# A static plan re-priced: new costs for small vector work, two due times and a buffer limit in a fused attention and MLP kernel

## The chip, the cores and the metric

One core of one Trainium2 chip. The metric is the device time of one execution in microseconds, the median over several runs. Engines are named as in the profile: PE is TensorE (PEld its weight loads), DVE VectorE, ACT ScalarE, POOL GpSimd, SP SyncE, which issues nearly all DMAs.

## The reference

Block-causal attention over 8 batches, 8 heads, 576 positions in blocks of 64, head size 64, followed by layer norm, a two-layer MLP with ReLU and a residual, all in float32:

```python
scores = scale * np.matmul(q, k.transpose(0, 1, 3, 2))
scores = np.where(block_i >= block_j, scores, -1000000000.0)
attn = softmax(scores); attn_out = np.matmul(attn, v)
x = attn_out.transpose(0, 2, 1, 3).reshape(8, 576, 512)
xn = (x - mu) / np.sqrt(var + 1e-06) * g_ln
out = x + np.maximum(xn @ w_ch1, 0.0) @ w_ch2      # 512 -> 2048 -> 512
```

## The kernel before

**Attention.** 32 pairs of heads, four to a batch (`pair`). The first block of 64 rows is kept out of a pair; the other 512 rows are four tiles of 128. A pair's PE work is: scores into PSUM (L416), transposes of the exponentials (L446), products with v (L452, L456). Between them DVE scales, masks and writes the scores to SBUF and finds each row's extreme in one instruction (L434, tiles `pu` for row tiles 1 and 2, `pab` for 3 and 4), ACT takes exp with row sums (L437), and ACT or DVE evacuates the transposes (`evac`, `copy` at L234 and L236). DVE transposes the finished rows (`ot`, L530) and SP stores them in `xd`.

**First blocks.** Once in 8 pairs, `first(m)` (m = 0 to 3) does the first blocks of two batches: scores of 64 x 64 (L568, on PE ahead of the scores of pair 8m + 4), maximum and difference on DVE (L576, L578, twice each), exp on ACT (L582), sum and reciprocal on DVE (L586 to L588, one task `total`), a product on POOL (L590), transposes (L597) and products with v (L608) on PE during pair 8m + 5, two transposes on DVE (L615), four stores. It loads `qk0` (L555) and `v0` (L571).

**Weights.** They come as 64-bit words of float64 patterns. `decode` runs 32 times (16 slices, each of both matrices): load `wr` (L345, L347), two ACT steps (L350, L355), a POOL step (L353), two DVE steps (L359, L362), then a store, for the second matrix after a split into a rounded high part and the rest (`wd`: cast at L234 or L236, L373 on POOL).

**Norm and MLP.** 36 row tiles in five rounds of 8, 8, 8, 8 and 4. `norm_tiles` handles two row tiles at a time (index q): load x from `xd`, scale by the softmax sums (L669), mean and variance (L691 in round 0, ACT in the others), reciprocal root (Newton steps on POOL), normalise (L724 in round 0), times g (L727, POOL), transpose (L729) through DRAM to `xt`. `operands` builds seven operand blocks `xm` from each `xt` for a seven-product (Strassen) scheme: differences (L754), casts to the rounded format (at L234 or L236) and remainders (L765). `products` (PE L867, evacuated and combined at L875, L880, L886, L887) and `second` (PE L927, added up at L936) run 8 groups in each round. `x` holds rows in rounds 1 to 4, `x0` in round 0.

**What orders the work.** Each engine runs its instructions in the order in which they are written, and that order comes from a planner (`Plan.run`) that simulates a time line while the kernel is built. Each task has a priority (smaller goes first), a modelled cost for every engine that could take it, and buffers it must find free. The planner takes the ready task with the smallest priority, on an engine only if no other engine would end it sooner, and on DVE and ACT it passes over a task if a task nearer by more than 100 is about to be ready before its modelled end. Pair k has priority 100 + 10k plus 0.05 for each step. PE's order in the attention phase is fixed by a chain of steps instead. Cost functions in us, n elements per partition:

```python
def dve(n):
    return .07 + n / 960
def act(n, sbuf=False):
    return .055 + .085 * sbuf + n / 1200
def pool(n):
    return .07 + n / 440
```

`D_0`, `D_1`, `LN_0`, `LN_1` and `LATER` (top of the file) set due times: decode n has the priority of pair `D_0 + D_1 * n + LATER` = 15 + 0.97n, the norm of round 0 that of pair 13 + 3q, its operands that of pair 25. Their loads wait for gates, the scores of earlier pairs (`ends`), in which LATER does not occur. `small` tiles share 21 buffers of 512 floats per partition, with a limit for each name: ya 10, x 3, t 4, tt 4, xnt 2, mag 2, sgn 2 and others.

Of the kernel before, what the change touches and what calls it, by code (L numbers as in the profile page):

```python
# [27 lines left out]
TILES = sum(ROUNDS)  # L28
D_0, D_1 = 12.0, .97
LN_0, LN_1 = 10, 3  # L30
LATER = 3
AHEAD = 100, 5, .25


# [23 lines left out]
class Plan:  # L58
# [5 lines left out]
    def add(self, eng, cost=None, fn=None, r=(), w=(), prio=0.0, size=0, alloc=(), mode=128):  # L64
        k = Task(eng if isinstance(eng, dict) else {eng: (cost, fn)}, prio, size)
        k.mode = mode
        before = {}
        for x in r:
            before.update(dict.fromkeys(x.writers))
        for x in w:  # L70
            before.update(dict.fromkeys(x.readers))
        for x in r:
            x.readers.append(k)
        for x in w:
            x.writers.append(k)
        for x in before:
            x.next.append(k)
        k.left = len(before)
        k.uses = list(dict.fromkeys(x.root for x in (*r, *w, *alloc)))
        for x in k.uses:  # L80
            x.users += 1
        k.allocs = [x for x in dict.fromkeys(x.root for x in (*w, *alloc)) if x.make]
        self.tasks.append(k)
        return k
# [105 lines left out]
# [6 lines that stand above are left out]


def pool(n):
    return .07 + n / 440

@with_exitstack
def attn_mlp_kernel(ctx: ExitStack, tc: tile.TileContext, qk, qk0, v, v0, w1, w2, g, out):
# [79 lines left out]
    def small(name, shape, dtype, most):  # L282
        return kind(name, shape, dtype, 21, None, "small", most)
# [8 lines left out]
    new_ot, new_v0 = small("ot", [P, 512], F32, 2), small("v0", [P, 512], F32, 1)  # L292
    new_e0, new_pt00, new_ot0 = (small(n, [P, 512], F32, 1) for n in ("e0", "pt00", "ot0"))
    new_mag, new_sgn = (small(n, [P, 512], I32, 2) for n in ("mag", "sgn"))
    new_ya, new_x, new_xnt = (small(n, [P, 512], F32, k) for n, k in (("ya", 10), ("x", 3), ("xnt", 2)))
    new_x0, new_xn = small("x0", [P, 512], F32, 2), small("xn", [P, 512], F32, 1)
    new_t, new_tt, new_sum = small("t", [P, 512], F32, 4), small("tt", [P, 2, 2, P], F32, 4), small("sum", [P, 2, 256], F32, 2)
    xs = [kind(f"xm{p}", [P, max(ROUNDS) // 2, 2, 2, P], F32R, 1)() for p in range(7)]
# [37 lines left out]
    def decode(j, second, prio, gate):  # L336
        n = 512
        wrb, magb, sgnb = new_word(), new_mag(), new_sgn()
        wr, mag, sgn = (lambda x=x: x.t for x in (wrb, magb, sgnb))
        wv = lambda i: wr().rearrange("p (n two) -> p n two", two=2)[:, :, i]  # L340
        word, magn, sign, full = (Buf(parent=x) for x in (wrb, magb, sgnb, sgnb))

        def dma():
            if second:
                nc.sync.dma_start(out=wr(), in_=w2[j])  # L345
            else:
                nc.sync.dma_start(out=wr().rearrange("p (c n) -> p c n", c=NC),  # L347
                                  in_=w1[:, :, 2 * j * P:2 * (j + 1) * P].rearrange("c p n -> p c n"))
        load(P * n * 8, dma, r=gate, w=[word], alloc=[wrb], prio=prio)
        add("ACT", act(n, True), lambda: nc.scalar.activation(  # L350
            out=mag().bitcast(F32), in_=wv(1).bitcast(F32), func=AF.Abs, scale=65536.0), r=[word], w=[magn], prio=prio)
        mag2 = Buf(parent=magb)
        add(any_of(lambda e: e.tensor_scalar_max(mag().bitcast(F32), mag().bitcast(F32), 2.0),  # L353
                   POOL=.07 + n / 367), r=[magn], w=[mag2], prio=prio)
        add("ACT", act(n, True), lambda: nc.scalar.activation(  # L355
            out=sgn(), in_=wv(0).bitcast(U32), func=AF.Copy, scale=2.0 ** -29 * (1 - 2.0 ** -9), bias=-0.499),
            r=[word], w=[sign], prio=prio)
        sign2 = Buf(parent=sgnb)
        add("DVE", dve(n), lambda: nc.vector.scalar_tensor_tensor(  # L359
            out=sgn(), in0=wv(1), scalar=-2147483648, in1=sgn(), op0=ALU.bitwise_and, op1=ALU.bitwise_or),  # L360
            r=[sign, word], w=[sign2], prio=prio)
        add("DVE", dve(n), lambda: nc.vector.scalar_tensor_tensor(  # L362
            out=sgn(), in0=mag(), scalar=3, in1=sgn(), op0=ALU.logical_shift_left, op1=ALU.bitwise_or),
            r=[sign2, mag2], w=[full], prio=prio)
        w = lambda: sgn().bitcast(F32)
        to = (wcs if second else w1f)[j // 2]
        out = Buf(parent=to)
        if second:
            wd = new_wd()
            hi, lo = Buf(parent=wd), Buf(parent=wd)  # L370
            add(any_of(lambda e: copy(e, wd.t[:, 0], w()), ACT=act(n, True), DVE=.12 + n / 1920),
                r=[full], w=[hi], prio=prio)
            add("POOL", pool(n), lambda: nc.gpsimd.tensor_sub(wd.t[:, 1], w(), wd.t[:, 0]), r=[full, hi], w=[lo], prio=prio)  # L373
            load(P * 4096, lambda: nc.sync.dma_start(
                out=to.t[:, 1024 * (j % 2):1024 * (j % 2) + 1024], in_=wd.t.rearrange("p l n -> p (l n)").bitcast(F32)),
                r=[hi, lo], w=[out], prio=prio)
        else:
            load(P * 2048, lambda: nc.sync.dma_start(out=to.t[:, 512 * (j % 2):512 * (j % 2) + 512], in_=w()),
                 r=[full], w=[out], prio=prio)
        whole.setdefault((second, j // 2), []).append(out)  # L380
# [164 lines left out]

    def first(m):

        prio = 100 + 10 * (8 * m + 3)
        step = [0]

        def pr():
            step[0] += 1
            return prio + .05 * step[0]
# [31 lines left out]
        def total():  # L585
            nc.vector.tensor_reduce(out=nm.t, in_=ev(e.t), op=ALU.add, axis=AX.X)  # L586
            nc.vector.tensor_scalar_add(nm.t, nm.t, 1e-9)
            nc.vector.reciprocal(nm.t, nm.t)  # L588
        add("DVE", dve(512) + .4, total, r=[p, *d], w=[r1], prio=pr())
        add("POOL", pool(512), lambda: nc.gpsimd.tensor_mul(  # L590
            ev(e.t), ev(e.t), nm.t.unsqueeze(2).to_broadcast([P, 8, 64])), r=[p, r1], w=[pn], prio=pr())
        tr, pt, turned_ = new_tr(), new_pt00(), Buf()
# [49 lines left out]
    def norm_tiles(n, q, prio, gate):  # L642
# [74 lines left out]
        for h, (x, part) in enumerate(rows):  # L717
            unit, scaled = Buf(parent=x), Buf(parent=x)
            if n:
                add("ACT", act(512, True), lambda x=x, h=h: nc.scalar.activation(  # L720
                    out=x.t, in_=x.t, func=AF.Identity, bias=norm.t[:, 10 + h:11 + h], scale=norm.t[:, 4 + h:5 + h]),
                    r=[rstd], w=[unit, *part], prio=prio)
            else:
                add("DVE", dve(512), lambda x=x, h=h: nc.vector.tensor_scalar(  # L724
                    out=x.t, in0=x.t, scalar1=norm.t[:, 2 * h:2 * h + 1], scalar2=norm.t[:, 4 + h:5 + h],
                    op0=ALU.subtract, op1=ALU.mult), r=[rstd], w=[unit, *part], prio=prio)
            add(any_of(lambda e, x=x: e.tensor_mul(x.t, x.t, g_sb), POOL=pool(512)), r=[unit, gb], w=[scaled], prio=prio)  # L727
            xnt, xw = new_xnt(), new_xw()
            add("DVE", dve(512), lambda x=x, xnt=xnt: nc.vector.transpose(xnt.t, x.t), r=[scaled], w=[xnt], prio=prio)  # L729
            parts = []  # L730
            for g4 in range(4):
                parts.append(Buf(parent=xw))
                load(32 * 2048, lambda xw=xw, xnt=xnt, g4=g4: nc.sync.dma_start(
                    out=xw.t[:, 32 * g4:32 * g4 + 32].rearrange("(k r) q -> r k q", r=32),
                    in_=xnt.t[32 * g4:32 * g4 + 32].rearrange("p (k q) -> p k q", q=32)), r=[xnt], w=[parts[-1]], prio=prio)
            half = Buf(parent=xt)
            load(P * 2048, lambda xw=xw, h=h: nc.sync.dma_start(
                out=xt.t[:, h].rearrange("p (c q) -> p c q", q=P), in_=xw.t.rearrange("(c p) q -> p c q", p=P)),
                r=parts, w=[half], alloc=[xt], prio=prio)
            ready.append(half)  # L740
# [4 lines left out]
    def operands(n, prio):  # L745
# [5 lines left out]

        def diff(p, q, i, in0, in1, r, w):
            new = Buf(parent=tts[q])
            add(any_of(lambda e: e.tensor_sub(tmp(q, i), in0(), in1()), DVE=dve(256), POOL=pool(256)),  # L754
                r=r, w=[new, *w], prio=prio + .1 * p + .01 * q)
            return new

        def split(step, p, q, src, r):
            old = held.get((n - 1, p), [])
            hi, lo = Buf(parent=xs[p]), Buf(parent=xs[p])  # L760
            three = lambda x: x.rearrange("p (c n) -> p c n", c=2)
            pr = prio + .1 * step + .01 * q
            add(any_of(lambda e: copy(e, xs[p].t[:, q, 0], three(src())), ACT=act(256, True), DVE=.08 + 256 / 1920),
                r=r, w=[hi, *old], prio=pr)
            add(any_of(lambda e: e.tensor_sub(xs[p].t[:, q, 1], three(src()), xs[p].t[:, q, 0]),  # L765
                       DVE=dve(256), POOL=pool(256)), r=[hi, *r], w=[lo, *old], prio=pr)
            got.setdefault(p, []).extend((hi, lo))
            return hi, lo

# [242 lines left out]
```

## Time and profile before

| | us |
|---|---|
| three runs | 1049.40, 1050.07, 1050.23 (median 1050.07) |
| the profiled execution's own time | 1050.46 |
| its span in the trace | 1048.7 |
| PE, DVE, ACT, POOL busy | 1037.1, 743.7, 524.0, 286.3 |

The attention phase lasts until about 303 us, the MLP's products from there to the end. The granted TensorE clock is at its full level throughout. Busy time is the time in which an engine has an instruction in work; for PE its ends are modelled, so an instruction that waits in PE's queue can look busy. The span leaves out what lies around the execution, some 1.8 us.

### The profile page before, as it was taken

How to read it: one execution, taken by the hardware profiler on the slowest of the kernel's cores; microseconds unless marked ns; L12 is line 12 of the kernel's file. 1: busy time of each engine (PE TensorE's matmuls, PEld its weight loads, DVE VectorE, ACT ScalarE, POOL GpSimd, SP SyncE). 2: the span in 40 equal slices, each digit the busy share in tenths (PEclk: the TensorE clock that was granted, in tenths of full speed). 3: DMA queues.
4: the chain of work that ended last, by engine and by line, in shares of the span. 5: the costliest groups of instructions: out<-in, count | busy, mean ns of one | idle time of the engine just before them, and what ended most of it. 6: DMA issues, size and time to landing. Idle time of an engine off the chain costs nothing.

```text
span 1048.7 us, 17977 instructions
## 1 busy us (share of the span) xinstructions
PE 1037.1 (99%) x6256; PEld 852.4 (81%) x6256; DVE 743.7 (71%) x1629; ACT 524.0 (50%) x1264; POOL 286.3 (27%) x468
## 2 busy tenths in 40 slices
PE   8999999999999999999999999999999999999998
PEld 7877777777878888888888888888888888888997
DVE  5778999989878878885656684665595555465544
ACT  6999888899875535342433341343242322122221
POOL 0223454545343765340222240222240220000000
PEclk9999999999999999999999999999999999999999
DMA  7578889898779898858777647688657667336873
GB/s 270 200 256 266 222 288 279 234 300 295 261 272 306 276 310 238 251 209 265 217 243 213 231 159 259 186 242 248 183 200 262 207 192 251 139 111 249 299 279 126
DMA packets 237930, 248.91 MB, mean 237 GB/s; under 512 B 159376, under 2 KB 188048, under 8 KB 227600
## 3 DMA queue, kind: packets, MB, share of 16 engines
q1 hardware_dynamic: 237840, 247.77, 72.9%
q8 instruction: 49, 0.80, 0.3%
q14 instruction: 41, 0.34, 0.1%
HBM read 182.71 MB, written 65.01 MB: 236 GB/s over the span
## 4 chain that ended last, share of the span: by engine, by line
PE 90%; DVE 7%; DMA 1%; issue 1%; ACT 0%; SPq 0%; POOL 0%; DVEq 0%; POOLq 0%; ACTq 0%
PE y L927 36%; PE p L867 32%; PE tr L446 7%; PE s L416 7%; PE o L456 5%; PE o L452 2%; DVE pab L434 1%; DMA wc<-wcs 1%; DVE pu L434 1%; DMA x<-xd 1%; DVE sgn L359 0%; DVE x L724 0%; DVE ya L936 0%; DVE xm L765 0%; PE tr L326 0%
## 5 line engine op out<-in xcount | busy, mean ns | idle before, releaser
L927 PE MATMUL y<-wc,h 128*128 128x512 f32 x1728 | 433.8, 390 | 0.2 <-DVE h L887 0.2
L927 PEld LDWEIGHTS y<-wc,h 128*128 128x128 f32 x1728 | 322.1, 188 | 66.4 <-DVE h L887 1.3
L936 DVE TENSOR_TENSOR ya<-y,ya 128x512 f32<-128x512 f32 x288 | 197.6, 687 | 181.6 <-PE y L927 178.8
L867 PE MATMUL p<-xm,wa 128*128 128x512 f32 (+1 forms) x960 | 221.7, 368 | 0.0
L867 PEld LDWEIGHTS p<-xm,wa 128*128 128x128 f32 x960 | 169.9, 188 | 31.5 <-issue 0.2
L867 PE MATMUL p<-xm,wb 128*128 128x512 f32 (+1 forms) x720 | 166.2, 368 | 0.0
L875 ACT COPY t<-p 128x512 f32<-128x512 f32 (+1 forms) x120 | 65.2, 544 | 167.8 <-PE p L867 166.0
L867 PEld LDWEIGHTS p<-xm,wb 128*128 128x128 f32 x720 | 127.7, 188 | 23.7
L886 ACT ACTIVATE h<-t 128x512 fp32r<-128x512 f32 (+1 forms) x120 | 62.2, 579 | 162.5 <-DVE t L880 162.3
L880 DVE TENSOR_TENSOR t<-p,t 128x512 f32<-128x512 f32 (+1 forms) x120 | 76.3, 636 | 47.9 <-PE p L867 43.2
L416 PE MATMUL s<-raw 64*128 64x224 f32 (+3 forms) x768 | 97.2, 388 | 2.5 <-DVE nm L434 2.0
L437 ACT ACTIVATE pab<-pab,nm 128x448 f32<-128x448 f32 (+1 forms) x128 | 91.2, 731 | 0.2 <-DVE nm L434 0.2
L234 ACT COPY pt<-tr 128x512 f32<-128x512 f32 x166 | 87.0, 597 | 7.2 <-PE tr L446 5.8
L416 PEld LDWEIGHTS s<-raw 64*128 64x128 f32 x768 | 74.8, 188 | 18.8 <-issue 5.1
L434 DVE CUSTOM_DVE_ANT_0 pab<-s,never 128x448 f32<-128x448 f32 (+1 forms) x128 | 82.7, 684 | 2.2 <-PE s L416 1.8
L456 PE MATMUL o<-pt,v 128*64 128x256 f32 (+1 forms) x768 | 80.1, 344 | 0.0
L456 PEld LDWEIGHTS o<-pt,v 128*64 128x64 f32 x768 | 55.3, 137 | 27.6
L887 DVE SCALAR_TENSOR_TENSOR h<-t,h 128x512 fp32r<-128x512 f32 (+1 forms) x120 | 74.1, 666 | 3.9 <-ACT h L886 3.8
L353 POOL TENSOR_SCALAR mag<-mag 128x512 f32<-128x512 f32 x32 | 48.7, 1525 | 101.4 <-ACT mag L350 92.4
L681 POOL TENSOR_SCALAR norm<-norm 128x1 f32<-128x1 f32 x28 | 6.9, 245 | 248.5 <-ACT xn L678 248.5
L437 ACT ACTIVATE pu<-pu,nm 128x320 f32<-128x320 f32 (+1 forms) x128 | 64.8, 510 | 19.5 <-DVE nm L434 18.5
L446 PE MATMUL tr<-ident,pab 128*128 128x128 f32 x512 | 63.3, 274 | 3.9 <-DVE nm L434 2.8
(96 smaller groups left out, 1036.3 us busy)
## 6 DMA issues: line engine op xcount, KB each, us to landing
wc<-wcs SPq DMA_DIRECT2D x40, 1024.0 KB, 7.0
wa<-was SPq DMA_DIRECT2D x32, 1024.0 KB, 6.3
wb<-wbs SPq DMA_DIRECT2D x32, 768.0 KB, 5.8
raw<-qk SPq DMA_DIRECT2D x32, 576.0 KB, 4.8
wr<-w SPq DMA_DIRECT2D x32, 512.0 KB, 6.1
v<-v SPq DMA_DIRECT2D x32, 320.0 KB, 5.5
x<-xd SPq DMA_DIRECT2D x144, 64.0 KB, 3.9
xrow<-x SPq DMA_DIRECT2D x36, 256.0 KB, 3.9
```

What stands on the lines that cost most here:

```text
L234: e.copy(out=out, in_=in_)
L416: nc.tensor.matmul(x, raw.t[HALF[h], 0, col], raw.t[HALF[h], 1, at:at + x.shape[1]], start=True, stop=True)
L434: add("DVE", dve(n) + .01, lambda: nc.vector.tensor_tensor_reduce(out=two(p.t[:, part(i, h)]), in0=mine(), in1=two(hide), scale=-0.125, sc ...
L437: add("ACT", act(n, True) + .14, lambda: nc.scalar.activation(out=p.t[:, part(i, h)], in_=p.t[:, part(i, h)], func=AF.Exp, bias=nm.t[:, at ...
L446: nc.tensor.transpose(o.t[:, n * P:(n + 1) * P], x, ident)
L456: nc.tensor.matmul(o.t[HALF[h], at + lo:at + 256], v_sb.t[:, ck, HALF[h]], rhs(h), start=False, stop=(n == len(steps) - 1), skip_group_che ...
L867: nc.tensor.matmul(x.t[:, 0:TN], w_(l), xs[m].t[:, 0:half, o, k], start=start and k == e == 0, stop=k == 1 and e == 2, skip_group_check=True)
L875: add("ACT", act(TN), lambda: nc.scalar.copy(out=t.t[:, 0:TN], in_=x.t[:, 0:TN]), r=[r], w=[new], prio=0)
L880: add("DVE", dve(TN), lambda: nc.vector.tensor_add(t.t[:, 0:TN], x.t[:, 0:TN], t.t[:, 0:TN]), r=r, w=[new], prio=0)
L887: add("DVE", dve(TN), lambda: nc.vector.scalar_tensor_tensor(out=x.t[:, 1, 0:TN], in0=src(), scalar=0.0, in1=x.t[:, 0, 0:TN], op0=ALU.max, ...
L927: nc.tensor.matmul(yb.t, x.t[:, l, at:at + P], wc.t[:, i, o], start=i == e == 0, stop=i == 1 and e == 2)
L936: add("DVE", dve(512), lambda yb=yb, ya=ya: nc.vector.tensor_add(ya.t, yb.t, ya.t), r=[part, before_], w=[now], prio=1)
```

## The change

Three cost functions change or are added (`pool`, `dve2` for DVE work from SBUF, `cast` for DVE casts to the rounded format), the cost of `total` grows, LATER goes from 3 to 2, the limit of `x` buffers from 3 to 4, and `first(m)` takes the priority of pair 8m + 4 in place of 8m + 3. The instructions themselves stay the same.

```diff
-LATER = 3
+LATER = 2
...
 def pool(n):
-    return .07 + n / 440
+    return .1 + n / 390
+def dve2(n):
+    return .1 + n / 760
+def cast(n):
+    return .2 + n / 1400
...
-    new_ya, new_x, new_xnt = (small(n, [P, 512], F32, k) for n, k in (("ya", 10), ("x", 3), ("xnt", 2)))
+    new_ya, new_x, new_xnt = (small(n, [P, 512], F32, k) for n, k in (("ya", 10), ("x", 4), ("xnt", 2)))
...   in decode, both steps (L359, L362)
-        add("DVE", dve(n), lambda: nc.vector.scalar_tensor_tensor(
+        add("DVE", dve2(n), lambda: nc.vector.scalar_tensor_tensor(
...   in first
-        prio = 100 + 10 * (8 * m + 3)
+        prio = 100 + 10 * (8 * m + 4)
...
-        add("DVE", dve(512) + .4, total, r=[p, *d], w=[r1], prio=pr())
+        add("DVE", dve(512) + .8, total, r=[p, *d], w=[r1], prio=pr())
...   in norm_tiles, round 0 (L724)
-                add("DVE", dve(512), lambda x=x, h=h: nc.vector.tensor_scalar(
+                add("DVE", dve2(512), lambda x=x, h=h: nc.vector.tensor_scalar(
...   in operands: diff (L754), the cast (L234, L236), the remainder (L765)
-            add(any_of(lambda e: e.tensor_sub(tmp(q, i), in0(), in1()), DVE=dve(256), POOL=pool(256)),
+            add(any_of(lambda e: e.tensor_sub(tmp(q, i), in0(), in1()), DVE=dve2(256), POOL=pool(256)),
...
-            add(any_of(lambda e: copy(e, xs[p].t[:, q, 0], three(src())), ACT=act(256, True), DVE=.08 + 256 / 1920),
+            add(any_of(lambda e: copy(e, xs[p].t[:, q, 0], three(src())), ACT=act(256, True), DVE=cast(256)),
...
-                       DVE=dve(256), POOL=pool(256)), r=[hi, *r], w=[lo, *old], prio=pr)
+                       DVE=dve2(256), POOL=pool(256)), r=[hi, *r], w=[lo, *old], prio=pr)
```

## Rows read from the trace of the kernel before

**Rows 1.** The page's head and its first part: the span, then busy us of each engine (share of the span) and number of instructions.

```profile
span 1048.7 us, 17977 instructions
PE 1037.1 (99%) x6256; PEld 852.4 (81%) x6256; DVE 743.7 (71%) x1629; ACT 524.0 (50%) x1264; POOL 286.3 (27%) x468
```

**Rows 2.** The order of time on PE in the attention phase: start us, length us, engine, line, operation, tiles, form, number of instructions merged. The row that begins the scores of a pair (L416) is shown for pairs 2, 12, 13, 16, 17, 20, 21, 26, 27 and 31, and the first-block scores (L568) ahead of pair 20.

```profile
19.88 2.86 PE L416 MATMUL s<-raw 64*128 64x320 f32 x24
...
110.25 0.80 PE L416 MATMUL s<-raw 64*128 64x320 f32 x2
...
120.40 2.86 PE L416 MATMUL s<-raw 64*128 64x320 f32 x24
...
148.45 2.86 PE L416 MATMUL s<-raw 64*128 64x320 f32 x24
...
157.19 2.86 PE L416 MATMUL s<-raw 64*128 64x320 f32 x24
...
184.55 0.69 PE L568 MATMUL tr<-qk 64*64 64x64 f32 x32
185.18 3.12 PE L416 MATMUL s<-raw 64*128 64x320 f32 x24
...
196.50 2.86 PE L416 MATMUL s<-raw 64*128 64x320 f32 x24
...
242.99 1.61 PE L416 MATMUL s<-raw 64*128 64x320 f32 x10
...
253.38 2.86 PE L416 MATMUL s<-raw 64*128 64x320 f32 x24
...
291.46 2.86 PE L416 MATMUL s<-raw 64*128 64x320 f32 x24
```

**Rows 3.** The chain of work that ended last, in order of time: start us, length us, engine, tile, line, number of instructions. First the transposes of a first-block job, then three places of the MLP phase.

```profile
124.28 0.44 PE tr L597 x4
...
369.38 2.72 PE y L927 x12
...
410.82 2.72 PE y L927 x12
...
941.22 2.72 PE y L927 x12
```

**Rows 4.** Three stretches: from:to and length us, then busy us (and instructions) of PE, PEld, DVE, ACT and POOL, the granted clock, the DMA engines' share and GB/s.

```profile
100.00:275.00 175.00, 170.08 (x1642) 133.43 (x1640) 161.61 (x479) 155.29 (x423) 84.10 (x118) 1.00 0.88 273
275.00:303.00 28.00, 28.00 (x282) 22.72 (x278) 21.93 (x65) 26.72 (x73) 8.38 (x7) 1.00 0.61 204
...
350.00:402.00 52.00, 51.82 (x228) 42.41 (x227) 45.89 (x71) 25.00 (x49) 34.73 (x40) 1.00 0.90 268
```

**Rows 5.** The order of time on DVE around the first-block jobs 1 and 2 (columns as in rows 2).

```profile
112.10 0.69 DVE L576 TENSOR_REDUCE nm<-tr 128x4 f32<-128x256 f32 x2
...
185.73 0.75 DVE L576 TENSOR_REDUCE nm<-tr 128x4 f32<-128x256 f32 x2
186.40 0.74 DVE L578 TENSOR_TENSOR e<-tr,nm 128x256 f32<-128x256 f32 x2
...
188.59 0.64 DVE L586 TENSOR_REDUCE nm<-e 128x8 f32<-128x512 f32 x1
...
190.05 0.13 DVE L539 TENSOR_SCALAR sums_all<-sums_all 128x32 f32<-128x32 f32 x1
...
191.06 0.45 DVE L434 CUSTOM_DVE_ANT_0 pu<-s,never 128x320 f32<-128x320 f32 x1
```

**Rows 6.** The order of time on DVE around the operand work of pair 25 and 26.

```profile
236.80 0.69 DVE L359 SCALAR_TENSOR_TENSOR sgn<-wr,sgn 128x512 int32<-128x512 int32 x1
237.40 0.62 DVE L434 CUSTOM_DVE_ANT_0 pab<-s,never 128x448 f32<-128x448 f32 x1
...
237.95 0.49 DVE L236 CAST xm<-xt 128x256 fp32r<-128x256 f32 x2
...
241.78 0.74 DVE L434 CUSTOM_DVE_ANT_0 pab<-s,never 128x576 f32<-128x576 f32 x1
```

**Rows 7.** First-block job 1 in the order of time on POOL and on PE; and the line of its `qk0` loads on SP: number, shortest/median/longest ns, first and last start us.

```profile
115.73 1.04 POOL L590 TENSOR_TENSOR e<-e,nm 128x512 f32<-128x512 f32 x1 [2.52 <-ACT pt L234]
...
124.12 0.60 PE L597 MATMUL tr<-ident,e 128*128 128x128 f32 x4
...
L555 SPq DMA_DIRECT2D qk<-qk x4: 328/427/795, 3.3 to 180.4; - x4
```

**Rows 8.** Groups of instructions by line and form: busy us, mean ns of one, idle before them. The two casts are those of 20 to 303 us; the next row is the work on `xm` alone from 100 to 275 us (columns as in rows 4); then the decode's first DVE step over the whole span.

```profile
L236 DVE CAST xm<-tt 128x256 fp32r<-128x256 f32 x12 | 5.1, 429 | 0.0
L236 DVE CAST xm<-xt 128x256 fp32r<-128x256 f32 x12 | 3.6, 332 | 0.0
...
100.00:275.00 175.00, 0.00 (x0) 0.00 (x0) 13.42 (x35) 1.54 (x4) 13.66 (x17) 1.00 0.88 273
...
L359 DVE SCALAR_TENSOR_TENSOR sgn<-wr,sgn 128x512 int32<-128x512 int32 x32 | 25.4, 795 | 1.7 <-ACT sgn L355 1.7
```

**Rows 9.** The page's DMA issues: tiles, queue, number, size, median us from issue to landing.

```profile
x<-xd SPq DMA_DIRECT2D x144, 64.0 KB, 3.9
```

**Rows 10.** The order of time on DVE and on POOL at 108 us.

```profile
108.57 3.19 POOL L727 TENSOR_TENSOR x<-x,g_sb 128x512 f32<-128x512 f32 x2 [1.59 <-DVE x L724]
108.86 1.76 DVE L359 SCALAR_TENSOR_TENSOR sgn<-wr,sgn 128x512 int32<-128x512 int32 x1
```

More of the change, by code (lines that the diff above doesn't have):

```diff
@@ L358, in decode @@
         sign2 = Buf(parent=sgnb)
-        add("DVE", dve(n), lambda: nc.vector.scalar_tensor_tensor(
+        add("DVE", dve2(n), lambda: nc.vector.scalar_tensor_tensor(
             out=sgn(), in0=wv(1), scalar=-2147483648, in1=sgn(), op0=ALU.bitwise_and, op1=ALU.bitwise_or),
             r=[sign, word], w=[sign2], prio=prio)
-        add("DVE", dve(n), lambda: nc.vector.scalar_tensor_tensor(
+        add("DVE", dve2(n), lambda: nc.vector.scalar_tensor_tensor(
             out=sgn(), in0=mag(), scalar=3, in1=sgn(), op0=ALU.logical_shift_left, op1=ALU.bitwise_or),
```

## The prediction

> **What bounds the kernel now.** I read the page first: TensorE (PE) is busy in nearly the whole span, so time can only be won where PE stands still or runs slower than its own pace [rows 1]. Busy time hides such places, since a matmul that waits inside its queue still counts. So I read the order of time on PE next and compared the starts of the score matmuls of successive pairs [rows 2]. A plain pair takes 157.19 - 148.45 = 8.74 us. A first-block job adds about 2.2 us to the pairs around it: 0.63 from its start to the next scores (185.18 - 184.55), twice 0.26 for scores that run 3.12 instead of 2.86, 0.44 for its transposes [rows 3], and for its values as much again as for its scores. From pair 2 (19.88) to pair 31 (291.46) that makes 29 x 8.74 + 4 x 2.2 = 262.3 us; the trace has 271.6. **About 9.3 us of waiting are in the attention phase.**
>
> In the MLP phase the chain of waits shows PE at an even pace: from 410.82 to 941.22 are exactly 26 x 20.40 us. Only from 369.38 to 410.82 it is 41.44, 0.64 over two periods [rows 3]. So the change can win 9.9 us at most, and not from rounds 1 to 4.
>
> What PE waits for is read from the stretches: from 100 to 275 us VectorE (DVE) is busy 161.6 of 175 us, ACT 155.3, POOL only 84.1 [rows 4]. Each engine runs in written order, so the wait is for whatever the planner put on DVE ahead of a softmax. The order of time on DVE shows two kinds. Behind the scores of pair 20 stand two L576 and two L578 (185.73 to 187.1) and L586 to L588 (188.59 to 190.05), between norm work, and the softmax of that pair starts at 191.06 [rows 5]; that interval is 196.50 - 185.18 = 11.32, less 8.74 + 0.26: 2.3 us lost. Job 1 likewise comes at 112.10 ahead of pair 12's softmax [rows 5], and 120.40 - 110.25 - 9.00 = 1.15 us are lost [rows 2]. The other kind is rounding and splitting of the MLP's operands: two casts at 237.95 open a run of them that ends at 241.78, where the pab softmax resumes [rows 6]; pair 26 takes 253.38 - 242.99 = 10.39, 1.65 too long [rows 2]. The remaining 9.3 - 2.3 - 1.15 - 1.65 = 4.2 us are smaller waits among the same work.
>
> **The change part by part.** No arithmetic is added or taken away. The parts are prices of the planner, two due times and a buffer limit.
>
> First-block job from 8m + 3 to 8m + 4. Old, its DVE steps were ahead of everything of pair 8m + 4 and of what was left of pair 8m + 3 (its evacuations and the ot transpose). New, they stand level with pair 8m + 4: by step numbers the two L576 and one L578 come before the third and fourth pu softmax, L586 to L588 after the third. So the leftovers and part of the softmax go first. What it can give is at most the two waits, 2.3 + 1.15 = 3.45; I take half for the part that stays in front, 1.7. At worst it costs: the job's POOL product ends at 116.8 and its transposes on PE start at 124.12 in a fixed place of PE's order [rows 7], 7.3 us of cover; a full pair later (8.74) would miss by 1.4, in four jobs 5.8. Level is not a full pair, so I take no loss. Its qk0 loads are issued at 3.3 to 180.4 us [rows 7]; the last of them, for job 3, goes out before job 2 has started (184.55, [rows 2]), eight pairs ahead of its use, so a delay of 10 priority units, one pair, is hidden. The v0 load and the four stores of its rows are moved past other SP work too; those rows belong to tiles 8, 17, 26 and 35, which no norm of round 0 reads, and the MLP covers them. Its one POOL product moves by no more than the DVE steps.
>
> Cast 256 from 0.213 to 0.383 us, ACT still 0.353. Between idle engines the planner now takes ACT. In the attention phase 24 of 28 of these casts ran on DVE, 5.1 + 3.6 = 8.7 us, and 4 on ACT at 1.54 / 4 = 0.385 us [rows 8]; ACT has 175 - 155.3 = 19.7 us idle in its busiest stretch [rows 4]. Moving half frees DVE of 4.3 us just in the runs that delay pair 26. Prices dve2 for the decode, the norm scaling and the operand differences (512: 0.603 to 0.774, 256: 0.337 to 0.437) and pool (512: 1.234 to 1.413) make the planner count 2 x 0.17 us more per decode and more room around each; the decode's first step has a mean of 0.795 [rows 8] and two POOL products beside it 3.19 / 2 = 1.6 [rows 10], so both come nearer. First-block total: 1.003 to 1.403, in the trace 190.05 - 188.59 = 1.46. Of the 1.65 + 4.2 = 5.85 us these prices can give anything between all and nothing, and ACT, on which exp and the evacuations run, can take some back; 24 casts at 0.385 us would be 9.2 us, half its idle time. I take a third, 2.0, because half of the casts leave but the L765 and the norm work stay.
>
> LATER from 3 to 2. Decode n competes from pair 14 + 0.97n instead of 15 + 0.97n, the norm of round 0 from pair 12 + 3q, its operands from pair 24. The loads (wr, x, the transposing stores and loads of xw) keep their gates, so SP's order moves by that due time alone. Per pair it is the same work; the whole stream slides by one pair. It is in front of a softmax sooner, though, and after 275 us there are 28 - 21.9 = 6.1 us idle on DVE [rows 4], so what slides out of that end was hidden and what slides in is not. Between a gain of one such wait (1.65) and a loss of one (1.65) I take a loss of a middle one, 0.2.
>
> Four x buffers. These serve rounds 1 to 4 alone. PE's even pace is the cover, so I count nothing. If it goes, because a fourth x takes one of 21 small tiles that the MLP's t needs, PE would wait for a row to arrive; the nearest row is a 3.9 us landing of x [rows 9], once a round 15.6 us. Below nothing it cannot help either, except in the 0.64 us.
>
> Sum: 1.7 + 2.0 - 0.2 = 3.5 us. The profiled execution took 1050.46 (span 1048.7 [rows 1], the rest lies around it), so 1046.96; it is 0.39 above the median of the runs, which makes **1046.6 us**.
>
> **A rule against it.** DVE's mean price is made of two prices. Unhindered, L359 at 236.80 gives way to the next instruction after 0.60 us, the old figure; behind a POOL product that began at 108.57 the same step takes 1.76 [rows 6, 10]. No single 0.774 is either. The Trainium skill (SBUF — State Buffer, "Who interferes with whom") says why: a DVE instruction with two SBUF inputs and a GpSimd instruction that reads SBUF exclude each other, and the later one stands still until the first is through. The trace agrees (1.76 against 0.60). By the mean the second term is 2.0; by two prices the plan stays wrong by -0.17 or +1 us at every step, and the term is about nothing.
>
> **The rivals.**
> A, the forecast: first-block steps and casts leave the front of the softmaxes, 2.2 to 6 us: 1044 to 1047.9. For it, the two waits with the job's own steps in front; against it, that the steps end up level and not behind. 0.43.
> B, the waits only move: the prices are means of free and blocked, so the new order finds other pairs to delay. First term 1.7, second nothing, LATER -0.2 or one more wait of 1.65: 1048.6 to 1050.2, and as a case 1048 to 1052. For it, DVE at 92% from 100 to 275 us, so that a delayed pair is never far. 0.28.
> C, nearly all of the 9.9 goes: 1040.5 to 1044. For it, ACT's and POOL's idle time; against it, that DVE keeps over 150 of 175 us. 0.15.
> D, slower: the dearer decode fits fewer gaps, and decodes pile up behind the attention phase, at 350 to 402 us, where DVE has 52 - 45.9 = 6.1 us free [rows 4]. A decode's two DVE steps at 0.795 [rows 8], with half of a wd cast (0.4, two of the casts of [rows 6]), are 1.8 us, an estimate; the fourth late decode decides, since 3.4 of them fill the gap. With seven late, 7 x 1.8 - 6.1 = 6.5 us of PE waiting against 3.5 won: 1053.1, and 1056.6 if nothing is won before. For it, that the planner puts off low-priority work when a nearer job is due; against it, LATER and the 6.1 us idle from 275 to 303. 0.14.
>
> **How the numbers follow.** Faster by over 0.2% (2.1 us, about what a measurement of this kernel can tell from no change) are A and C, 0.58; within it B, 0.28; slower D, 0.14. The range leaves out D and the far half of C: 1042 to 1051.8. The full cost of the x buffers and of four late transposes lies in what is left out. A alone would be 1044 to 1047.9.
>
> **What would show it.** Right: pair 12's and pair 20's intervals near 9.0 us, L576 after the ot transpose of pair 8m + 3 and no longer ahead of both pu softmaxes; at least 10 of the 28 xm casts of the attention phase on ACT; the first product of the MLP 3 to 4 us sooner, and 20.40 us a period after it. Wrong: the sum of waits of pairs 2 to 31 still near 9 us with other pairs in it (B), a stretch at 350 to 402 longer by more than 0.64 us with more L359 behind 303 us than now (D), or a wait of PE's transposes L597 for POOL (the first term's lower end).

## The result: slower, with less waiting in the attention phase and more in the MLP phase

After takes 1060.06 us in the median (8 runs, 1054.26 to 1063.45), before beside it 1049.85 (8 runs, 1049.05 to 1051.52): a ratio of 1.0087, 95% interval 1.0069 to 1.0105. The profiled execution of after took 1055.96, at the lower end of its runs; what the median loses beyond that (4.1 us) no profile shows. Line numbers of after are 9 above those of before from the decode on (L359 is now L368, L416 is L425, L927 is L936).

The page's head of after answers to [rows 1]: the span grew by 5.5 us, PE's busy time by 2.2, and its share stays at 99%. Busy time does not show where the loss is.

```profile
span 1054.2 us, 18020 instructions
PE 1039.3 (99%) x6256; PEld 852.4 (81%) x6256; DVE 734.3 (70%) x1585; ACT 529.2 (50%) x1287; POOL 297.5 (28%) x489
```

**Attention phase.** The order of time on PE, the scores of pairs 2, 12, 13, 20, 21, 22 and 31 (columns as in [rows 2]):

```profile
18.82 2.86 PE L425 MATMUL s<-raw 64*128 64x320 f32 x24
...
109.34 3.12 PE L425 MATMUL s<-raw 64*128 64x320 f32 x24
119.36 2.86 PE L425 MATMUL s<-raw 64*128 64x320 f32 x24
...
183.54 3.12 PE L425 MATMUL s<-raw 64*128 64x320 f32 x24
192.53 3.40 PE L425 MATMUL s<-raw 64*128 64x320 f32 x24
204.49 3.12 PE L425 MATMUL s<-raw 64*128 64x320 f32 x24
...
288.28 2.86 PE L425 MATMUL s<-raw 64*128 64x320 f32 x24
```

Pair 31 starts 3.18 us sooner than in [rows 2], but pair 2 already 1.06 sooner (18.82 against 19.88). That start is not the change's: the kernel that is after with three x buffers has it at 19.99 (the last section has the cause). From pair 2 on, 2.1 us are won up to pair 31, and 2.47 up to the first `y` product (319.06 - 19.88 = 299.18 before, 315.53 - 18.82 = 296.71 after). Pair 20's interval is 8.99 now, its 2.3 us of [rows 2] are gone, and pair 21's, plain before, is 11.96: 2.15 above 8.74 + 1.07.

**MLP phase.** The chain of waits, the runs of twelve `y` products:

```profile
315.53 2.72 PE y L936 x12
...
386.25 2.72 PE y L936 x12
...
495.53 2.72 PE y L936 x12
...
515.93 2.72 PE y L936 x12
...
558.23 2.72 PE y L936 x12
...
701.03 2.72 PE y L936 x12
...
742.71 2.72 PE y L936 x12
```

The places are read against the grid of before: its 410.82 of [rows 3] lies 91.76 after its first `y` at 319.06, and all later ones whole periods of 20.40 on. After's 495.53 lies 180.00 behind its first `y`, the grid has 91.76 + 4 x 20.40 = 173.36: **6.64 us lost by then**, none before 386.25 (70.72, three periods and the 9.52 with which both begin). From 515.93 to 558.23 are 42.30, 1.50 over two periods; from 701.03 to 742.71 are 41.68, 0.88 over. The sum, 9.02, is all of it: 729.6 us from first `y` to the end before, 738.7 after. The third place, 0.88, was not followed. 9.0 lost, 2.5 and the 1.06 of the start won: 5.5.

What PE waits for at the first place, in the order of time on SP, DVE and PE of after:

```profile
395.70 0.67 SPq L746 DMA_DIRECT2D xt<-xw  x1
...
400.71 10.15 SPq L742 DMA_DIRECT2D xw<-xnt  x8
```
```profile
412.49 0.43 DVE L763 TENSOR_TENSOR tt<-xt 128x256 f32<-128x256 f32 x1 [4.78 <-DMA xw<-xnt]
...
416.03 1.89 DVE L896 SCALAR_TENSOR_TENSOR h<-t,h 128x512 fp32r<-128x512 f32 x3
```
```profile
416.42 0.73 PE L936 MATMUL y<-wc,h 128*128 128x512 f32 x2 [1.61 <-ACT h L895]
```

DVE stands 4.78 us at an operand difference of round 1. The row itself had come: its two `xt` loads went out at 394.36 and 395.70 and had landed by 400.48. What DVE waits for is a buffer. In this program that `tt` is placed in the small buffer in which an `xnt` was, and the step waits for the semaphores of the four stores that read this `xnt`. They are the second half of a burst of eight that took SP 10.15 us (eight such stores take 4.15 at 514), and the last of them lands at 412.37. ACT stood 3.71 us until 411.12 in the same way, at an `xn` in the buffer of the other `xnt`. Behind the step, in DVE's written order, stand `ya`, `t` and `h` of the running round, and PE stands for `h`. Up to 1.7 of the 6.64 us are the lower clock that follows (last section), an estimate.

At the second place it is a row that is late: SP issues 3 and 11 loads of `x` before the second `xt`, POOL waits for it (it lands at 544.87), DVE for POOL, PE for DVE's `h`.

```profile
529.73 5.40 SPq L669 DMA_DIRECT2D x<-xd  x3
...
535.74 5.81 SPq L669 DMA_DIRECT2D x<-xd  x11
541.60 0.49 SPq L746 DMA_DIRECT2D xt<-xw  x1
```
```profile
545.04 0.74 POOL L763 TENSOR_TENSOR tt<-xt 128x256 f32<-128x256 f32 x1 [6.29 <-DMA xt<-xw]
```
```profile
545.81 0.43 DVE L763 TENSOR_TENSOR tt<-xt,tt 128x256 f32<-128x256 f32 x1 [1.75 <-POOL tt L763]
```
```profile
547.50 1.19 PE L936 MATMUL y<-wc,h 128*128 128x512 f32 x4 [1.19 <-DVE h L896]
```

The decode moved as well. Its first DVE step by stretch (length us, busy and number, clock, DMA share, GB/s), before and then after:

```profile
303.00:402.00 99.00, 8.87 (x10) 1.00 0.91 290
402.00:470.00 68.00, 0.00 (x0) 1.00 0.73 239
```
```profile
303.00:402.00 99.00, 7.34 (x9) 1.00 0.94 295
402.00:470.00 68.00, 2.25 (x3) 0.97 0.78 259
```

Twelve of 32 come after 303 us instead of ten, three of them after 402 where before had none.

### The profile page after: what moved, and what is told of

The parts are those of the page before. It is cut to its first block, busy times and chain, and to the rows that moved or that the text cites. A ratio compares the mean times of both kernels' runs of the same rounds, so it can differ in the third digit from the quotient of the medians.

```text
span 1054.2 us, 18020 instructions
## 1 busy us (share of the span) xinstructions
PE 1039.3 (99%) x6256; PEld 852.4 (81%) x6256; DVE 734.3 (70%) x1585; ACT 529.2 (50%) x1287; POOL 297.5 (28%) x489
## 4 chain that ended last, share of the span: by engine, by line
PE 89%; DVE 4%; DMA 2%; POOL 2%; SPq 2%; issue 1%; ACT 0%; POOLq 0%; DVEq 0%; ACTq 0%
PE y L936 34%; PE p L876 30%; PE tr L455 8%; PE s L425 8%; PE o L465 6%; PE o L461 3%; SPq L669 1%; DMA wa<-was 1%; DMA v<-v 1%; DVE h L896 1%; DVE xm L774 0%; DVE pab L443 0%; DMA x<-xd 0%; POOL x L736 0%; PE tr L335 0%
## 5 line engine op out<-in xcount | busy, mean ns | idle before, releaser
L936 PE MATMUL y<-wc,h 128*128 128x512 f32 x1728 | 434.7, 391 | 3.6 <-DVE h L896 2.0
L936 PEld LDWEIGHTS y<-wc,h 128*128 128x128 f32 x1728 | 322.8, 189 | 71.8 <-DVE h L896 4.3
L425 PE MATMUL s<-raw 64*128 64x224 f32 (+3 forms) x768 | 96.6, 385 | 1.3 <-DVE nm L443 1.1
L425 PEld LDWEIGHTS s<-raw 64*128 64x128 f32 x768 | 74.5, 187 | 17.2 <-issue 4.7
L446 ACT ACTIVATE pu<-pu,nm 128x192 f32<-128x192 f32 (+1 forms) x128 | 65.2, 517 | 17.7 <-DVE nm L443 17.1
L455 PEld LDWEIGHTS tr<-ident,pab 128*128 128x128 f32 x512 | 56.6, 140 | 2.6 <-issue 0.9
```

Source lines behind the costliest of these rows:

```text
L425: nc.tensor.matmul(x, raw.t[HALF[h], 0, col], raw.t[HALF[h], 1, at:at + x.shape[1]], start=True, stop=True)
L446: add("ACT", act(n, True) + .14, lambda: nc.scalar.activation(out=p.t[:, part(i, h)], in_=p.t[:, part(i, h)], func=AF.Exp, bias=nm.t[:, at ...
L455: nc.tensor.transpose(o.t[:, n * P:(n + 1) * P], x, ident)
L936: nc.tensor.matmul(yb.t, x.t[:, l, at:at + P], wc.t[:, i, o], start=i == e == 0, stop=i == 1 and e == 2)
```

## The experiments

All times in one table: median and ratio to before of the same chip; then from one profiled execution of each what the attention phase (pair 2's scores to the first `y`) and the MLP phase (first `y` to the end) take more than before's 299.18 and 729.6, and how many decodes start after 303 us.

| kernel | median us | ratio (95%) | attention | MLP | late decodes |
|---|---|---|---|---|---|
| after | 1060.06 | 1.0087 (1.0069-1.0105) | -2.5 | +9.0 | 12 |
| a_x3: after, three x buffers | 1050.43 | 1.0012 (1.0002-1.0021) | -2.1 | +1.8 | 13 |
| a_oldprice: after, all prices old | 1061.27 | 1.0108 (1.0091-1.0125) | +4.0 | +6.8 | 10 |
| b_x4: before, four x buffers | 1056.93 | 1.0071 (1.0056-1.0087) | -1.0 | +7.1 | 9 |
| b_price: before, all prices new | 1054.21 | 1.0046 (1.0031-1.0061) | -2.3 | +6.7 | 13 |
| b_later2: before, LATER 2 | 1050.89 | 1.0008 (0.9998-1.0018) | +0.8 | -0.6 | 10 |
| b_first4: before, job at 8m + 4 | 1051.31 | 1.0016 (1.0005-1.0028) | -0.4 | +2.2 | 11 |
| p_att: new prices, attention work | 1058.42 | 1.0076 (1.0052-1.0100) | -2.4 | +11.4 | 13 |
| p_mlp: new prices, other work | 1049.32 | 0.9995 (0.9985-1.0005) | -0.2 | -0.6 | 9 |
| dec_only: dve2 in the decode | 1056.30 | 1.0065 (1.0050-1.0080) | -0.9 | +8.6 | 13 |
| price_nodec: new prices, decode's DVE steps old | 1060.06 | 1.0102 (1.0084-1.0119) | +6.4 | +5.1 | 11 |
| b_x4_late: before, four x from round 2 | 1050.41 | 1.0005 (0.9995-1.0014) | +0.1 | +0.1 | 10 |
| b_x4_s22: b_x4, 22 small tiles | 1060.23 | 1.0104 (1.0086-1.0122) | +2.0 | +11.1 | 10 |
| a_x4_late: after, four x from round 2 | 1052.14 | 1.0021 (1.0012-1.0031) | +0.1 | +2.2 | 13 |
| a_x3_first3: a_x3, job at 8m + 3 | 1072.26 | 1.0209 (1.0192-1.0226) | +0.2 | +21.6 | 13 |
| a_x3_cast0: a_x3, old price of the cast | 1075.38 | 1.0240 (1.0225-1.0256) | +1.8 | +23.6 | 13 |
| a_x3_later3: a_x3, LATER 3 | 1074.59 | 1.0239 (1.0213-1.0264) | -2.3 | +25.0 | 14 |
| a_x3_d11: a_x3, decodes due one pair sooner | 1058.17 | 1.0076 (1.0056-1.0096) | +6.9 | +1.9 | 13 |
| dec_sooner: dec_only, due two pairs sooner | 1062.57 | 1.0114 (1.0099-1.0129) | -0.1 | +12.4 | 13 |

Some of the expectations below give 726 us for the MLP phase of before and 15 late decodes for all new prices. The traces have 729.6 and 13.

### Which part costs: the x buffers, from both ends

a_x3 is after with this edit, b_x4 is before with its reverse:

```
-    new_ya, new_x, new_xnt = (small(n, [P, 512], F32, k) for n, k in (("ya", 10), ("x", 4), ("xnt", 2)))
+    new_ya, new_x, new_xnt = (small(n, [P, 512], F32, k) for n, k in (("ya", 10), ("x", 3), ("xnt", 2)))
```

> The change with the x limit put back to 3. Theory SP-burst (the fourth x buffer lets the row loads of x run ahead in bursts on SP, in front of the xt loads; DVE waits for xt in order with PE's evacuations behind it): the MLP phase goes back to the 726 us from its first y product to the end that it took before, the attention phase keeps its 3.5 us, 1046 to 1048. Theory prices (the new costs reorder the norm and operand work of rounds 1 to 4): still 1055 or more, MLP near 735.

> The kernel before with the x limit at 4 and nothing else. Theory SP-burst: the MLP phase alone loses 5 to 13 us, 1055 to 1063, attention as before (first y product at 319 us). Theory prices: no difference that can be measured, 1050.

Taken out of after, the fourth buffer gives back 9.0 - 1.8 = 7.2 us of the MLP phase and all but 0.12% of the whole; put alone into before it costs 7.1 there. The two ends agree. In b_x4 all of it lies between the `y` at 326.61 and that at 415.90, while round 0 runs and round 1's rows are made. What PE waits for there, on ACT, on SP and on PE:

```profile
398.51 0.63 ACT L678 ACTIVATE xn<-x 128x512 f32<-128x512 f32 x1 [7.92 <-issue]
...
399.65 1.67 ACT L886 ACTIVATE h<-t 128x512 fp32r<-128x512 f32 x3
```
```profile
386.03 6.88 SPq L733 DMA_DIRECT2D xw<-xnt  x3
393.01 2.37 SPq L737 DMA_DIRECT2D xt<-xw  x1
395.42 0.50 SPq L733 DMA_DIRECT2D xw<-xnt  x1
```
```profile
400.85 0.73 PE L927 MATMUL y<-wc,h 128*128 128x512 f32 x2 [1.82 <-ACT h L886]
403.13 0.96 PE L927 MATMUL y<-wc,h 128*128 128x512 f32 x3 [1.55 <-DVE h L887]
```

ACT stands 7.92 us at the first norm step of a row of round 1, with PE's `h` behind it. The view names no releaser, but the trace has what the step waits for: the semaphores of four stores of one `xnt`, three of them issued in the 6.88 us from 386.03 and the fourth, behind a load, at 395.42. The fourth lands at 398.29, 0.2 us before the step starts, and in this program the step's `xn` is placed in the buffer of that `xnt`. So it is the wait of the first place of after again: a small buffer that a store still reads. Between 340 and 440 us of before no wait of DVE or ACT ends with a DMA. PE's own columns show 3.4 us of the 7.1; the lower clock that follows is up to 1.7 more, an estimate (last section); the rest is in no column.

b_x4_late keeps three `x` for round 1 and gives rounds 2 to 4 four of their own; a_x4_late is a_x3 with the same edit:

```
+    new_xl = small("xl", [P, 512], F32, 4)
...
-            x = new_x() if n else new_x0()
+            x = (new_x() if n == 1 else new_xl()) if n else new_x0()
```

and b_x4_s22 is b_x4 with one more small tile:

```
-        return kind(name, shape, dtype, 21, None, "small", most)
+        return kind(name, shape, dtype, 22, None, "small", most)
```

> The kernel before with a limit of 3 x buffers for the rows of round 1 and 4 for those of rounds 2 to 4. Theory crowding (a fourth buffer brings norm work of round 1 forward into 303 to 400 us, where DVE is busy nine tenths): as before, 1050. Theory SP-burst in every round: MLP still loses 3 or more, 1053 or more.

> The change with a limit of 3 x buffers for the rows of round 1 and 4 for rounds 2 to 4. Theory crowding in round 1: all of the loss that x 4 brings goes, 1050 to 1051 as with 3 buffers throughout. Theory that the fourth buffer also costs in rounds 2 and 3 (the waits near 540 and 720 us of the changed kernel): 1053 or more.

> The kernel before with 4 x buffers and 22 small tiles in place of 21. Theory that the fourth x only takes a small tile from others (t, ya, tt): the loss goes, 1050. Theories crowding and SP-burst: the loss stays, 1055 or more.

Four buffers from round 2 on cost nothing (b_x4_late), and in after this removes 7.9 of the 10 us: the cost is round 1's rows alone. The 22nd small tile did not help; it gives the planner another order, and that loses 11.1. In that order ACT stands 8.92 us in the same way, at a `sgn` in the buffer of an `xnt` (SP; ACT):

```profile
387.64 9.90 SPq L733 DMA_DIRECT2D xw<-xnt  x4
```
```profile
400.21 0.66 ACT L355 ACTIVATE sgn<-wr 128x512 int32<-128x512 uint32 x1 [8.92 <-DMA xw<-xnt]
```

So one tile more does not remove the wait. With four buffers more of round 1's row work is let in among round 0's matmuls (in b_x4 its third to eighth transposes come 3.6 to 17.8 us sooner than in before), its stores come where SP is slow, and an engine is held at a buffer that the planner's time line has as free.

### The other parts, one at a time

b_later2 and b_first4 are before with the one and the other of these edits:

```
-LATER = 3
+LATER = 2
```
```
-        prio = 100 + 10 * (8 * m + 3)
+        prio = 100 + 10 * (8 * m + 4)
```

a_oldprice is before with both and four `x`; b_price is before with the rest of the change's diff, the lines of `pool`, `dve2`, `cast` and `+ .8`.

> The change with all old prices (pool, dve2, cast and total), keeping LATER 2, x 4 and the first-block job at 8m + 4. Theory SP-burst: MLP still loses 5 or more, 1053 to 1062. Theory prices: MLP back to 726 us, total 1047 to 1050.

> The kernel before with the new prices alone. Theory SP-burst: the MLP phase stays at 726 us and the attention phase wins about 2 us by the moved casts, 1048. Theory prices: MLP loses 5 to 10 us, 1054 to 1060.

> The kernel before with LATER 2 alone. Both theories leave the MLP phase alone up to 1 us (726 us from first y product). If the due time is what cost the kernel with old prices 4 us of its attention phase, first y product at 322 to 324 us and 1053 to 1055; if it is the first-block job, 319 and 1050.

> The kernel before with the first-block job at the priority of pair 8m + 4 alone. As predicted: 1.7 us won in the attention phase, 1048.3; if the job is what cost 4 us with old prices: first y product at 322 to 324 us, 1053 to 1055.

LATER alone is nothing that can be measured. The job a pair behind wins 0.4 us in the attention phase and loses 2.2 in the MLP phase. The prices win 2.3 and lose 6.7. The 4.0 us that a_oldprice loses in the attention phase are in neither part alone (+0.8 and -0.4) and stay open. Alone, the x buffers, prices and job lose 7.1 + 6.7 + 2.2 = 16 us in the MLP phase; together they lose 9.0: the parts don't add.

### Inside the prices: the decode

dec_only is before with this edit at both DVE steps of the decode, and price_nodec is b_price with its reverse:

```
-        add("DVE", dve(n), lambda: nc.vector.scalar_tensor_tensor(
+        add("DVE", dve2(n), lambda: nc.vector.scalar_tensor_tensor(
```

p_att has the new prices in the decode, the first-block job and the norm and operands of round 0 alone, p_mlp in weight preparation and rounds 1 to 4 alone; the cast in p_att, for one:

```
-            add(any_of(lambda e: copy(e, xs[p].t[:, q, 0], three(src())), ACT=act(256, True), DVE=.08 + 256 / 1920),
+            add(any_of(lambda e: copy(e, xs[p].t[:, q, 0], three(src())), ACT=act(256, True), DVE=(cast(256) if n == 0 else .08 + 256 / 1920)),
```

> New prices for the work of the attention phase alone (decode, first-block job, norm and operands of round 0), old prices for the weight preparation and rounds 1 to 4; due times and x as before. Theory that the MLP's own work is re-ordered by its prices: first y product at 315 to 316, MLP back to 730 us of span, 1046 to 1047. Rival, decodes put off out of the attention phase: MLP still 735, 1052.

> The complement: new prices for weight preparation and for norm and operands of rounds 1 to 4 alone. Theory that the MLP's own work is re-ordered: first y product at 319, MLP 735 to 737, 1055 to 1057. Rival, late decodes: 1050.

> The kernel before with the decode's two DVE steps priced by dve2 and nothing else. Theory late decodes (the dearer decode is put off out of the attention phase: 10 of 32 first steps after 303 us before, 15 with all new prices, the last at 391 against 427 us): 13 or more behind 303 us, first y product at 315 to 317, MLP 735 or more, 1053 to 1058. Rival, the other new prices of the attention phase (casts, differences, norm, first-block total): as before, 10 decodes behind 303 us, 1050.

> All new prices except dve2 in the decode, due times and x as before. Theory late decodes: 10 or 11 decodes behind 303 us, MLP back to 729 to 731; the attention phase loses the part of its gain that came from the decodes missing in it, first y product at 317 to 319: 1047 to 1050. Rival: as with all new prices, 1054.

The prices of rounds 1 to 4 do nothing (p_mlp); the loss comes with those of the attention phase's own work (p_att, +11.4), and 8.6 of it with the decode alone (dec_only), which has 13 late decodes. Why a dearer decode is put off: on DVE and ACT the planner passes over a task of a priority above 100 when a task whose priority is smaller by more than 5, half a pair (not by 100, as the description of the kernel has it), will be ready 0.25 us or more before the first one's modelled end. A modelled end at 0.774 instead of 0.603 us lets more such tasks come first. In dec_only 8.3 us of the loss lie between the `y` runs at 367.29 and 498.62. DVE's order there:

```profile
404.11 0.69 DVE L364 SCALAR_TENSOR_TENSOR sgn<-wr,sgn 128x512 int32<-128x512 int32 x1
...
405.91 0.68 DVE L885 TENSOR_TENSOR t<-p,t 128x512 f32<-128x512 f32 x1
406.51 0.68 DVE L364 SCALAR_TENSOR_TENSOR sgn<-wr,sgn 128x512 int32<-128x512 int32 x1
```

and on ACT, some 40 us later, a cast that waits for decoded weights to be loaded back:

```profile
448.04 0.41 ACT L239 CAST wb<-wf 128x256 fp32r<-128x256 f32 x1 [6.35 <-DMA wf<-w1f]
```

Two decodes stand between the evacuations of round 0, and a weight tile comes late. How the 8.3 us divide between these is not shown, and the number of late decodes does not order the losses: a_x3, a_x4_late and a_x3_d11 have 13 as well and lose about 2 us in the MLP phase, and price_nodec loses 5.1 with 11. And price_nodec shows the other side: with the decodes left where they were, the other new prices lose 6.4 us in the attention phase, although 17 of the 28 `xm` casts run on ACT there. What the prices win in the attention phase, they win only together with decodes put off.

### What holds the loss down: the other three parts, taken back one at a time

a_x3_first3, a_x3_cast0 and a_x3_later3 are a_x3 with one of these each:

```
-        prio = 100 + 10 * (8 * m + 4)
+        prio = 100 + 10 * (8 * m + 3)
```
```
-            add(any_of(lambda e: copy(e, xs[p].t[:, q, 0], three(src())), ACT=act(256, True), DVE=cast(256)),
+            add(any_of(lambda e: copy(e, xs[p].t[:, q, 0], three(src())), ACT=act(256, True), DVE=.08 + 256 / 1920),
```
```
-LATER = 2
+LATER = 3
```

> The change with 3 x buffers and the first-block job back at 8m + 3 (new prices and LATER 2 stay). As predicted for the job: 1.7 us lost, 1052. Rival, the job's due time does nothing since its steps stay level with the pair: within 1 us of 1050.4.

> The change with 3 x buffers and the old price of the casts (0.213 on DVE), so that they go back from ACT to DVE. As predicted (casts off DVE win 2 us): first y product 1.5 to 2 us later, 1052. Rival, the attention phase was won by decodes put off and the casts did nothing or harm: first y product within 1 us of 317.1 or earlier, 1049 to 1050.5.

> The change with 3 x buffers and LATER back at 3 (new prices and first-block job at 8m + 4 stay). Theory that LATER 2 makes up for the dearer prices: more decodes behind 303 us than 13, MLP 736 or more, 1054 to 1058. Rival, LATER does nothing here: 1050 to 1051.

Each of them, taken out of a kernel that is 0.12% slower than before, costs 2% and more. Two have one place. In a_x3_first3 the last transposes of round 1's rows (`xnt`) come at 469.10 us, 33 us later than in before (435.9). By then SP's order has a store of finished output ahead of each store of a transpose, and those wait for the evacuations; the last `xw` goes out at 480.69, the last `xt` at 486.11, and PE, done with round 0, stands for operands (SP; DVE; PE):

```profile
474.01 0.30 SPq L742 DMA_DIRECT2D xw<-xnt  x1
474.68 0.36 SPq L948 DMA_DIRECT2D out_t<-ya  x1
...
480.69 0.97 SPq L742 DMA_DIRECT2D xw<-xnt  x2
486.11 0.38 SPq L746 DMA_DIRECT2D xt<-xw  x1
```
```profile
489.02 0.43 DVE L763 TENSOR_TENSOR tt<-xt 128x256 f32<-128x256 f32 x1 [13.00 <-DMA xt<-xw]
```
```profile
485.11 0.79 PE L876 MATMUL p<-xm,wa 128*128 128x512 f32 x1 [9.83 <-ACT xm L243]
490.04 6.50 PE L876 MATMUL p<-xm,wa 128*128 128x512 f32 x17 [4.13 <-DVE xm L774]
```

In a_x3_cast0 the last transpose comes at 470.5 and PE stands 11.59 and 3.52 us for the same operands. In a_x3_later3 it comes at 446.3; its waits are smaller and many between 400 and 475 us, and no one step stands out. Why a different price of a cast delays those rows by 30 us is open too.

### Decodes due sooner

a_x3_d11 is a_x3 with this edit, dec_sooner is dec_only with 10.0 in that place:

```
-D_0, D_1 = 12.0, .97
+D_0, D_1 = 11.0, .97
```

> The change with 3 x buffers and the decodes one pair sooner still (D_0 11 in place of 12). Theory late decodes: 10 or 11 decodes behind 303 us, MLP 729 to 730 where 3 buffers alone had 731.4, the attention phase loses up to 2 us: 1048 to 1051. If the attention phase keeps its gain: 1047. Rival, decodes late or not are no cause: 1050.4 and 13 behind 303 us.

> The dearer decode alone (dve2 in its two DVE steps), with its due time two pairs sooner (D_0 10 in place of 12), norm and operands as before. Theory late decodes: with the decodes back before 303 us (10 or 11 behind it) the MLP's loss goes, 729 to 731 in place of 738, and with it the gain of the attention phase: 1049 to 1052. Rival, the price costs in another way than by lateness: 14 or fewer behind 303 us and MLP still 736 or more, 1055.

Neither brought the decodes back: 13 are late in both, and a_x3_d11 pays 9.0 us more than a_x3 in the attention phase (6.9 + 2.1). So the lateness could not be parted from the price. That it is the lateness which costs is inferred from its place alone, and the counts of the table do not bear it out. No kernel was faster than before beyond what can be told apart.

## Why the prediction was wrong

**Four x buffers: the step that failed.** It said "PE's even pace is the cover, so I count nothing"; the term measured 7.2 us. The pace of [rows 3] is a result of the order of DVE, ACT and SP, not slack: in 350 to 402 us DVE had 6.1 us left of 52 and the DMA engines ran at 0.90 [rows 4]. The buffers were said to serve rounds 1 to 4, and I looked for their cost in those; they begin to serve when round 1's rows are made, in round 0's time, and that is where the 7.1 us of b_x4 were lost, half of the step's own upper end (15.6). Behind that end stood a small tile taken from the MLP's `t` and a row for which PE waits. The traces have something near it: an engine held at a small buffer that a store of `xnt` still reads (DVE 4.78 us in after, ACT 7.92 in b_x4), with the evacuations behind it. One tile more did not cure it (b_x4_s22).

**First-block job: 1.7 forecast.** Pair 12's wait went from 1.15 to 1.02, pair 20's 2.3 to pair 21: 0.3 won, in b_first4 0.4 in the whole phase. DVE's order of after shows why:

```profile
183.67 0.73 DVE L585 TENSOR_REDUCE nm<-tr 128x4 f32<-128x256 f32 x2
184.31 0.75 DVE L587 TENSOR_TENSOR e<-tr,nm 128x256 f32<-128x256 f32 x2
...
185.53 0.43 DVE L443 CUSTOM_DVE_ANT_0 pu<-s,never 128x320 f32<-128x320 f32 x1
...
189.44 0.68 DVE L595 TENSOR_REDUCE nm<-e 128x8 f32<-128x512 f32 x1
```

In this job L585 and L587 stand ahead of all four `pu` softmaxes still (in job 1 they stand among them, as foreseen); only L595 to L597 went behind. It was rival B for this term.

**Prices: 2.0 forecast, 2.3 measured in the attention phase (b_price), for a wrong reason: the size was luck.** The casts did move, 15 of 28 to ACT from 100 to 303 us (at least 10 were forecast), but this frees nothing by itself, as price_nodec's +6.4 shows. ACT's groups in that stretch, which answer to [rows 8]:

```profile
L243 ACT CAST xm<-tt 128x256 fp32r<-128x256 f32 x8 | 3.2, 414 | 4.1 <-POOL tt L763 4.0
L243 ACT CAST xm<-xt 128x256 fp32r<-128x256 f32 x7 | 2.9, 408 | 0.0
```

The longest first decode step fell from 1.765 to 1.367 us, its median is 0.69 in after: free and hindered steps still differ by a factor of two. The one of 1.367 starts at 56.53, beside a POOL product that runs from 56.08 to 57.35. That agrees with the Trainium skill (SBUF — State Buffer, "Who interferes with whom"), by which the later of two such instructions waits for the earlier one. By one mean the term was 2.0, by two prices nothing, and neither reckoning had the MLP phase in it.

**LATER: -0.2 forecast;** alone 1.0008 (0.9998 to 1.0018). Right within what can be told, though with three x buffers and the new prices it decides over 2%, which no term of the sum could hold.

**The sum** for the attention phase was 3.5; 2.5 came, from other terms than were added up. After that the text took "20.40 us a period" as given. It holds in all but three places of after, and these cost 9.0.

**Rival D** had the right sign, and dearer decodes are put off into round 0 and cost (dec_only 1.0065); that their lateness is what costs is not shown. Its place was wrong: 402 to 470 us, not 350 to 402, where after is on the grid still until 386.25. Its price was wrong in kind: I summed DVE's busy time against free time, and after's DVE is less busy in 402 to 470 than before's (second row before):

```profile
402.00:470.00 68.00, 64.19 (x270) 50.91 (x269) 54.00 (x92) 28.84 (x65) 38.29 (x49) 0.97 0.78 259
```
```profile
402.00:470.00 68.00, 68.00 (x301) 56.32 (x300) 55.81 (x106) 29.27 (x64) 29.93 (x52) 1.00 0.73 239
```

What cost, where it could be followed, was an engine standing still at a step whose data or buffer came late. In the whole change the x buffers account for 7.2 of the 9.0; how the decode's loss is nearly made up by the job, LATER and the cast's price (a_x3 1.8 against 6.7 of b_price) stays open.

## What to carry to other kernels

Even pace of the bound engine is no slack: ask what each in-order engine would stand at if one load or store came 5 us later, and count the evacuations queued behind that step. A store that reads a buffer holds it until it has landed, so a late store stops an engine that has its data. A larger buffer limit is a change of order from the moment its first user is prepared, which may be a whole round before that user computes. In a planned order parts don't add, so a change of several prices is tried part by part, and taken out part by part too: both ends agreed for the x buffers here, and for nothing else.

## What was not expected of the hardware

Issuing a 64 KB transfer on SP took 0.49 us each at 535.74 (5.81 for 11, so 0.53 with the gaps) and 1.80 in a burst at 529.73 (5.40 for 3); eight `xw` took 4.15 at 514 and 10.15 at 400.71, where the DMA share of 400 to 425 us was 0.95. The price of an issue in the planner is one number.

After PE had stood, the granted clock fell from its full level (2.4 GHz) to the lower one (1.2). In after PE stood 1.61 and 0.22 us for `h`, and from 417.68 to 421.09 the clock was at half. The 22 `y` products from 417.37 took 6.90 us; at the pace of twelve in 2.72 they take 4.99, an estimate. The stretch on PE (busy us and products, the clock, the DMA share, GB/s):

```profile
417.68:421.09 3.41, 3.41 (x9) 0.50 1.06 324
```

All fourteen kernels here that are slower than before by 0.2% or more have such a fall before their last 3 us; before, a_x3, b_later2, b_first4, p_mlp and b_x4_late have none. It lasts 3.4 us in all in after, b_x4, b_price, dec_only and a_x4_late, and 20.5 in a_x3_first3, where PE is busy in 9.3 of them. Half of PE's busy time in it, 1.7 to 4.6 us in these, is the clock's and not a wait's, an estimate. It also parts kernels that are alike there: a_x4_late has its fall at 199.13, in the attention phase, where a_x3 has none.

And the first 32 scores took 3.72 us in after and 4.67 in before, with nothing of the change in front of them. The trace's record of the full clock begins at 4.67 us in after, but at 6.90 in before (so "throughout" in the section on the time before holds from there on). From the first score on, 1.95 us hold eleven score matmuls in before and nineteen in after. Half of 1.95 is 0.98, an estimate, against the 0.95 measured. This record begins between 4.29 and 7.44 us in the twenty traces, so 1 us of an interval that starts at 0 belongs to the execution.
